# Weighted values of a windowed attention: FP32 products of PSUM weights, pair additions and gate products on GpSimd

## The chip, the cores and the metric

One core of one Trainium2 chip. The metric is the device time of the kernel in microseconds (us), median of several runs; the span in a profile, from the first to the last instruction, is about 2 us shorter. In the text PE is the matmul engine, DVE the vector engine, ACT the scalar engine and GpSimd (POOL in the profile) the fourth compute engine. PSUM (PS in the listings) is the memory in which PE's results land, used here in 8 banks; the other tiles named are in SBUF, the second memory of the core that the engines work on: VX holds values, ATX the softmax weights, PA to PC products of the two, SV added products, OT weighted values, HT hidden products, USX up projections, LOG and SM the softmax.

## The reference, cut to what matters

```python
# x: 2048 x 640, 32 heads of 20, window of 8 keys at distances 0, 2, ..., 14
xn = layernorm(x)
qkv = xn @ wqkv
attn = softmax(einsum("bhsd,bhswd->bhsw", q, kg) * scale)   # 8 weights a position
o = einsum("bhsw,bhswd->bhsd", attn, vg)                     # "weighted values"
# the second branch; its gate has no nonlinearity
h = (xn @ w_gate) * (xn @ w_up)                              # 2048 x 1536
return x + o @ wo + h @ w_down
```

## The kernel before: the parts that matter

The sequence is cut into 4 blocks of 512 positions. All instructions are put into one program order, and each engine works through its own part of it strictly in order (in after, a DVE product that could have run at 172.4 us stood until 177.05 behind a final addition that waited 4.23 us, see e13); semaphores are made from the buffers that operations share. The work of the second half is:

- 20 *units* of weighted values, 5 for each block of 512 positions. A unit multiplies 4 x 2 x 512 values by weights on DVE. The 128 partitions are 4 window groups x 32 heads, the factor 2 is the pair of *offset groups* (window positions 4 apart, called r), and PE sums the groups with a matrix of ones, 32 rows of output for each of 4 head dimensions.
- Gate and up projections: 24 groups of 5 matmuls a block on PE, evacuated by ACT, and 12 *gate products* a block (gate x up).
- The down projection of a block, 8 tiles of 17 matmuls. It needs the block's 12 gate products and its 5 units. I call the four dn0 to dn3.

```python
    def pv_mul(u):                                  # one DVE operation, bf16, both inputs in SBUF
        j = u // NCH
        v, p = VX[:, u % NVX], PB[u % NP]           # NP = 3 product buffers
        vw = bass.AP(v.tensor, v.offset, [v.ap[0], [VW, 4], [8, 2], [1, JB]])
        at = ATX[:, :, j * JB:(j + 1) * JB]
        a = at.unsqueeze(1).to_broadcast([128, 4, 2, JB])
        op("dve", lambda e: e.tensor_tensor(p[:], vw, a, ALU.mult), ...)

    def pv_sum(us):                                 # 16 matmuls for a pair of units
        for u in us:
            for r in range(2):
                for dq in range(4):                 # start at r == 0, stop at r == 1
                    op("pe", ... e.matmul(o, SEL[:], p[:, dq, r, :], ..., tile_position=(0, 32 * dq)))
        # ... ACT copies the sums into OT

    # what PE does, in this order; a small clock in the program decides
    # where the units and head sums are put between these entries
    add_gu(0); add_gu(1); add_dn(0); add_gu(2); add_dn(1); add_gu(3); add_dn(2); add_dn(3)
```

The hidden products live in two buffers (`HT[:, j % 2]`), so the gate groups of block 2 can't start before dn0 has read block 0. The up projections wait in 6 small buffers (`USX`) for their gate product.

Of the kernel before, what the change touches and what calls it, by code (L numbers as in the profile page):

```python
# [3 lines left out]
FP32 = mybir.dt.float32  # L4
BF16 = mybir.dt.bfloat16
ACT = mybir.ActivationFunctionType
ALU = mybir.AluOpType
# [3 lines left out]
NCH = 5  # L11
# [10 lines left out]
JB = 512  # L22
# [5 lines left out]
VW = JB + 8  # L28
# [9 lines left out]
class Sched:  # L38
# [47 lines left out]
    def op(self, eng, fn, r=(), w=(), dma=False, name=""):  # L86
        X = _Op()
        X.eng, X.fn, X.name, X.dma = eng, fn, name, dma
        X.needs_tick, X.event, X.pre_know, X.idx = False, None, None, len(self.ops)
        rk = [k for a in r for k in self.keys(a)]  # L90
        wk = [k for a in w for k in self.keys(a)]
        deps = {}
        inorder = eng in ("pe", "act", "dve")
        for k in rk:
            st = self.state.get(k)
            if st is not None and st[0] is not None:
                deps[st[0].idx] = st[0]
        for k in wk:
            st = self.state.get(k)
            if st is None:  # L100
                continue
            o, rds = st
            if o is not None and not (eng == "pe" and o.eng == "pe"):
                deps[o.idx] = o
            for q in rds:
                if inorder and q.eng == eng and not q.dma:
                    continue
                deps[q.idx] = q
        last = {}
        keep = []  # L110
        for d in deps.values():
            if d.dma or d.eng == "pool":
                keep.append(d)
            else:
                b = last.get(d.eng)
                if b is None or b.idx < d.idx:
                    last[d.eng] = d
        X.deps = keep + list(last.values())
        for d in X.deps:
            if not d.dma:  # L120
                d.needs_tick = True
        for k in rk:
            st = self.state.get(k)
            if st is None:
                self.state[k] = [None, [X]]
            elif inorder and st[1] and st[1][-1].eng == eng and not st[1][-1].dma:
                st[1][-1] = X
            else:
                st[1].append(X)
        for k in wk:  # L130
            self.state[k] = [X, []]
        if dma:
            X.event = (self.nc.alloc_semaphore(f"dma{self.n_dma}"), 16)
            self.n_dma += 1
        self.ops.append(X)
        return X
# [59 lines left out]
def build_kernel(nc, A_x, A_wqkv, A_wo, B_x, B_w_gate, B_w_up, B_w_down, out):  # L196
    K = Sched(nc)
    op = K.op
# [3 lines left out]
    def sb(name, shape, dtype=BF16, at=None):  # L202
        n = mybir.dt.size(dtype)
        for s in shape[1:]:
            n *= s
        n = (n + 63) // 64 * 64
        if at is None:
            at = place[0]
            place[0] += n
        assert at + n <= 229344, (name, at + n)  # L210
        return K.sbuf(name, shape, dtype, at)
# [9 lines left out]
    a_qk = place[0]  # L221
    place[0] += 2 * DH * VW * 2
    QT = sb("QT", [128, NCH, S], at=a_qk)
    KT = sb("KT", [128, NCH, VL], at=a_qk + NCH * S * 2)
    NVX = 8
    VX = sb("VX", [128, NVX, 4, VW], at=a_qk)
    a_ra = place[0]
    HT = sb("HT", [128, 2, NF, JB])
    WQKV = sb("WQKV", [128, 3, NCH, D], at=a_ra)
    a_pr = place[0]  # L230
    NPW = 6
    PRD = sb("PRD", [128, NPW, S])
    PB = [sb("PA", [128, 4, 2, JB], at=a_pr), sb("PB", [128, 4, 2, JB], at=a_pr + 8 * JB * 2),
          sb("PC", [128, 4, 2, JB], at=a_qk + NVX * 4 * VW * 2)]
    NP = len(PB)
    ATX = sb("ATX", [128, 2, S], at=a_pr + 2 * 8 * JB * 2)
    MX = sb("MX", [128, 4, JB], at=a_pr)
    MY = sb("MY", [128, 2, JB], at=a_pr + 4096)
# [20 lines left out]
    SEL = sb("SEL", [128, 32])  # L259
    G = sb("G", [128, NCH, H])  # L260
    PS = nc.alloc_psum_tensor("PS", [128, 8, 512], FP32)
# [6 lines left out]
    def dma(o, i, r=(), w=(), name="", eng="sp"):  # L268
        return op(eng, lambda e: e.dma_start(o, i), r=r, w=w, dma=True, name=name)  # L269
# [7 lines left out]
       r=[IDENT[:]], w=[IDENT[:]], name="ident")  # L277
# [3 lines left out]
       r=[G[:]], w=[G[:]], name="g1")  # L281
    op("pool", lambda e: e.affine_select(G[:], G[:], pattern=[[128, NCH], [-DH, H]], compare_op=ALU.is_ge,
                                         fill=0.0, base=0, channel_multiplier=1),
       r=[G[:]], w=[G[:]], name="g2")
# [89 lines left out]
    bank_ring = list(range(6))  # L374
# [116 lines left out]
    def attn_move(j):  # L491
        for wq in range(4):
            src = LOG[32 * j:32 * j + 32].rearrange("p (r q) s -> p r q s", r=2)[:, :, wq, :]
            dst = ATX[32 * wq:32 * wq + 32, :, j * JB:(j + 1) * JB]
            dma(dst, src, r=[src], w=[dst], name=f"atx{j}_{wq}")
# [5 lines left out]
        dma(dst, src, r=[("vscr", m, q) for m in range(NCH + 1) for q in range(4)], w=[dst], name=f"vx{u}")  # L501


    def pv_mul(u):
        j = u // NCH
        v, p = VX[:, u % NVX], PB[u % NP]
        vw = bass.AP(v.tensor, v.offset, [v.ap[0], [VW, 4], [8, 2], [1, JB]])
        at = ATX[:, :, j * JB:(j + 1) * JB]
        a = at.unsqueeze(1).to_broadcast([128, 4, 2, JB])
        op("dve", lambda e: e.tensor_tensor(p[:], vw, a, ALU.mult), r=[v, at], w=[p[:]], name=f"pv{u}")  # L510
        if u + NVX < NU:
            vx_load(u + NVX)

    def pv_sum(us):
        for u in us:
            b, p = 6 + u % 2, PB[u % NP]
            for r in range(2):
                for dq in range(4):
                    o = PS[32 * dq:32 * dq + 32, b, :]
                    op("pe", (lambda o, p, dq, r: lambda e: e.matmul(o, SEL[:], p[:, dq, r, :], start=(r == 0), stop=(r == 1),  # L520
                                                                  tile_position=(0, 32 * dq)))(o, p, dq, r),
                       r=[SEL[:], p[:, dq, r, :]], w=[o], name=f"I{u}_{dq}_{r}")
        for u in us:
            j, c = divmod(u, NCH)
            b = 6 + u % 2
            o = OT[:, c, j * JB:(j + 1) * JB]
            op("act", (lambda o, b: lambda e: e.activation(o, PS[:, b, :], ACT.Copy))(o, b), r=[PS[:, b, :]], w=[o],  # L527
               name=f"oev{u}")
# [2 lines left out]
    pair_ctr = [0]  # L531
    h_pending = []
    h_keep = [1]

    def flush_h(keep):
        n = 0
        while len(h_pending) > keep:
            h_pending.pop(0)()
            n += 1
        return n  # L540

    def glu(which, m, j):
        k = pair_ctr[0] % NUS
        T = (WG, WU)[which]
        h = HT[:, j % 2, m, :]
        o = (h, USX[:, k, :])[which]
        b = bank()
        for c in range(NCH):
            l, x = T[:, c, m * 128:(m + 1) * 128], XNT[:, c, j * JB:(j + 1) * JB]
            op("pe", (lambda l, x, c: lambda e: e.matmul(PS[:, b, :], l, x, start=(c == 0), stop=(c == NCH - 1)))(l, x, c),  # L550
               r=[l, x], w=[PS[:, b, :]], name=f"gu{which}_{m}_{j}_{c}")
        op("act", lambda e: e.activation(o, PS[:, b, :], ACT.Copy), r=[PS[:, b, :]], w=[o], name=f"guev{which}_{m}_{j}")  # L552
        if which == 1:
            pair_ctr[0] += 1
            h_pending.append(lambda: op("dve", lambda e: e.tensor_tensor(h, h, o, ALU.mult), r=[h, o], w=[h],  # L555
                                        name=f"h{m}_{j}"))
            return 0.43 * flush_h(h_keep[0])
        return 0.0

    def xr_load(t):  # L560
# [58 lines left out]
    for t0 in (0, 2):  # L619
        bm = bank()  # L620
        for which in (0, 1):
            for t in (t0, t0 + 1):
                b = bank()
# [8 lines left out]
    for t0 in (4, 6, 8, 10):  # L632
        bm = None
        for g in range(5):
            b = bank()
# [12 lines left out]
    NU = NJ * NCH  # L648
    t_pe, t_dve = [40.0], [41.0]
# [3 lines left out]
    for q in range(4):  # L653
        a, b = SEL[32 * q:32 * q + 32, :], IDENT[32 * q:32 * q + 32, 32 * q:32 * q + 32]
# [14 lines left out]
    units_done = [0]  # L669
# [17 lines left out]
    def run_fill(until):  # L687
        while t_pe[0] < until and pos[0] < len(fill):
            it = fill[pos[0]]
            if it[0] == "dn":  # L690
                if units_done[0] < NCH * (it[1] + 1):
                    return
                t_pe[0] += 2.31
                it[2]()
            else:
                t_pe[0] += it[0]
                d = it[1]()
                t_dve[0] += d if isinstance(d, float) else 0.0
            pos[0] += 1
# [4 lines left out]
    batch, ready = [], None  # L704
    for i, (w, c) in enumerate(order):
# [6 lines left out]
        if ready is not None and len(batch) == 2:  # L712
# [6 lines left out]
            ready = None  # L719
        if len(batch) == 4:  # L720
            ready = (batch, t_dve[0] + 0.2)
# [4 lines left out]
    t_dve[0] = max(t_dve[0], t_pe[0] + 2.5)  # L726
    for u in range(NVX):
        vx_load(u)
    bank_ring[:] = bank_ring + [4, 5]
    h_keep[0] = NUS - 1  # L730
    for cost, st in softmax_steps():
        st()
# [2 lines left out]
    h_keep[0] = 1  # L735
    for j in range(NJ):
        attn_move(j)
    t_dve[0] += 3.0
    for u in range(0, NU, 2):
        pv_mul(u)  # L740
        if u:
            run_fill(t_ready)
            pv_sum((u - 2, u - 1))
            t_pe[0] = max(t_pe[0], t_ready) + 1.13
            units_done[0] += 2
        pv_mul(u + 1)
        t_dve[0] += 4.57
        t_ready = t_dve[0] + 0.2
    run_fill(t_ready)
    pv_sum((NU - 2, NU - 1))  # L750
    units_done[0] += 2
    while pos[0] < len(fill):
        run_fill(1e9)
    K.emit(stores)
# [35 lines left out]
```

## Time and profile before

| | before |
|---|---|
| device time | 289.2 us |
| PE busy | 275.4 of 287.3 us |
| DVE busy, GpSimd busy | 171.4, 2.3 us |
| product of one unit (DVE) | 2.29 us |
| dn0 starts | 146.95 us |

The page's first parts, kernel before: busy time and share of the span for each engine, then the span in 40 slices of 7.2 us with the busy share in tenths, and the clock granted to PE.

```profile
PE 275.4 (96%) x1968; PEld 156.7 (55%) x1986; DVE 171.4 (60%) x260; ACT 116.1 (40%) x211; POOL 2.3 (1%) x17
...
PE   7899999999999999998997999999999999999996
...
DVE  5776792999999768859994999521222112222221
...
POOL 2000000000000000000000000000000000000000
PEclk9999999999999999999999799999999999999999
```

PE is the limit; counted from 0, DVE is full in slices 7 to 12, where it multiplies queries and keys, and again in most of 18 to 24 (about 129 to 180 us), where the units run; GpSimd does next to nothing.

Costliest groups, kernel before, by form: engine, operation, output<-inputs, partitions x elements, count, then busy us, mean ns, and idle time before them with its releaser.

```profile
L432 DVE TENSOR_TENSOR PRD<-QT,KT 128x2048 bf16<-128x2048 bf16 x40 | 45.8, 1220 | 5.0 <-ACT KT L390 4.2
...
L510 DVE TENSOR_TENSOR PA<-VX,ATX 128x4096 bf16<-128x4096 bf16 x7 | 16.0, 2285 | 4.0 <-DMA ATX<-LOG 4.0
...
L555 DVE TENSOR_TENSOR HT<-HT,USX 128x512 bf16<-128x512 bf16 x48 | 19.1, 420 | 39.5 <-ACT USX L552 39.5
```

Windows, kernel before, one for each stage of PE (end of softmax; rest of block 1; dn0; block 2; dn1).

```profile
105.00:125.00 20.00, 19.95 (x93) 9.10 (x93) 15.11 (x20) 14.04 (x21) 0.00 (x0) 1.00 0.27 85
125.00:147.00 22.00, 20.64 (x128) 8.56 (x129) 21.41 (x21) 11.67 (x22) 0.00 (x0) 1.00 0.66 195
147.00:175.00 28.00, 25.89 (x218) 15.30 (x218) 24.24 (x20) 5.73 (x11) 0.00 (x0) 0.94 0.54 158
175.00:203.00 28.00, 27.68 (x149) 11.97 (x150) 11.47 (x15) 16.35 (x28) 0.00 (x0) 1.00 0.04 12
203.00:222.00 19.00, 18.95 (x139) 13.60 (x139) 4.19 (x9) 0.60 (x1) 0.00 (x0) 1.00 0.16 53
```

The columns are the window, its length, then busy us (and instructions) of PE, PE's weight loads, DVE, ACT and GpSimd, the granted clock, the DMA share and GB/s. Up to dn0 (second line) PE and DVE are both almost full; afterwards DVE has more and more room, and PE loses only about 2 us in the dn0 stage.

Two moments of the timeline of before (start, duration, engine, operation): a softmax step, and dn0's first 12 matmuls.

```profile
115.07 1.22 DVE L455 TENSOR_TENSOR SM<-LOG 128x1024 f32<-128x1024 bf16 x1
...
146.95 1.79 PE L576 MATMUL PS<-WD,HT 128*128 128x320 bf16 x12
```

### The profile page before, as it was taken

The page shows a single profiled execution, that of the slowest core. Times are in us where ns is not written, and L with a number is a line of the kernel's source. Part 1 is how long each engine was busy: PE and PEld are TensorE (multiplying, and loading weights), DVE is VectorE, ACT ScalarE, POOL GpSimd, SP SyncE. Part 2 cuts the span into 40 slices and gives each one's busy share as a digit, 9 for nine tenths or more (in the row PEclk, how much of TensorE's full clock was granted, in tenths as well). Part 3 has the DMA queues.
Part 4 walks back from the last instruction along what each step waited for, and adds up shares of the span by engine and source line. Part 5 has one row for each costly group of instructions (what it writes and reads, how often), then busy time and mean ns, then how long its engine had stood idle before and what let it go on. Part 6 is the DMA issues. An engine that isn't in the chain of part 4 may idle for free.

```text
span 287.3 us, 4706 instructions
## 1 busy us (share of the span) xinstructions
PE 275.4 (96%) x1968; PEld 156.7 (55%) x1986; DVE 171.4 (60%) x260; ACT 116.1 (40%) x211; POOL 2.3 (1%) x17
## 2 busy tenths in 40 slices
PE   7899999999999999998997999999999999999996
PEld 3789887443434344443453564444676444677774
DVE  5776792999999768859994999521222112222221
ACT  2355556544644479525732034655200555300000
POOL 2000000000000000000000000000000000000000
PEclk9999999999999999999999799999999999999999
DMA  6824999007989692035976731000021100012211
GB/s 199 281 72 66 396 389 256 3 2 302 392 335 391 217 356 65 0 76 140 307 221 190 208 105 50 2 0 0 2 91 48 46 0 0 2 63 73 74 43 46
DMA packets 30468, 39.57 MB, mean 138 GB/s; under 512 B 4464, under 2 KB 26608, under 8 KB 30448
## 3 DMA queue, kind: packets, MB, share of 16 engines
q1 hardware_dynamic: 30448, 39.29, 41.5%
q8 instruction: 15, 0.25, 0.3%
q14 instruction: 5, 0.04, 0.0%
HBM read 25.07 MB, written 13.16 MB: 133 GB/s over the span
## 4 chain that ended last, share of the span: by engine, by line
PE 72%; DVE 15%; DMA 4%; issue 4%; ACT 2%; SPq 2%; DVEq 0%; ACTq 0%
PE PS L550 27%; PE PS L576 19%; PE PS L385 11%; PE PS L404 7%; PE PS L440 3%; DVE PC L510 3%; DVE PB L510 3%; DMA XST<-in_A_x_dram 2%; PE PS L397 2%; DVE PA L510 2%; SPq L269 2%; DVE SM L455 2%; DMA XR<-in_A_x_dram 1%; PE PS L360 1%; DVE RS L468 1%
## 5 line engine op out<-in xcount | busy, mean ns | idle before, releaser
L550 PE MATMUL PS<-XNT,WU 128*128 128x512 bf16 x238 | 59.4, 379 | 1.4 <-ACT USX L552 1.2
L576 PE MATMUL PS<-WD,HT 128*128 128x320 bf16 x384 | 59.0, 304 | 0.0
L550 PE MATMUL PS<-XNT,WG 128*128 128x512 bf16 x229 | 57.5, 379 | 0.7 <-issue 0.5
L432 DVE TENSOR_TENSOR PRD<-QT,KT 128x2048 bf16<-128x2048 bf16 x40 | 45.8, 1220 | 5.0 <-ACT KT L390 4.2
L576 PEld LDWEIGHTS PS<-WD,HT 128*128 128x128 bf16 x384 | 37.8, 99 | 17.2 <-issue 1.7
L552 ACT ACTIVATE HT<-PS 128x512 bf16<-128x512 f32 x48 | 29.1, 605 | 39.6 <-PE PS L550 39.6
L580 DVE TENSOR_TENSOR FOUT<-PS,XR 128x320 bf16<-128x320 f32 x32 | 15.4, 490 | 46.2 <-PE PS L576 42.5
L555 DVE TENSOR_TENSOR HT<-HT,USX 128x512 bf16<-128x512 bf16 x48 | 19.1, 420 | 39.5 <-ACT USX L552 39.5
L550 PEld LDWEIGHTS PS<-XNT,WU 128*128 128x128 bf16 x240 | 23.3, 98 | 30.1 <-ACT USX L552 1.7
L552 ACT ACTIVATE USX<-PS 128x512 bf16<-128x512 f32 x48 | 28.9, 603 | 26.3 <-PE PS L550 18.3
L550 PEld LDWEIGHTS PS<-XNT,WG 128*128 128x128 bf16 x240 | 22.9, 98 | 29.5 <-issue 1.7
L385 PE MATMUL PS<-XNT,WQKV 128*128 128x512 bf16 x145 | 32.8, 379 | 0.4 <-issue 0.3
L576 PE MATMUL PS<-WO,OT 128*128 128x320 bf16 x160 | 27.1, 300 | 0.0
L385 PEld LDWEIGHTS PS<-XNT,WQKV 128*128 128x128 bf16 x150 | 14.1, 98 | 18.8 <-ACT VST L390 2.1
L404 PE MATMUL PS<-XNT,WQKV 128*128 128x256 bf16 x200 | 23.6, 273 | 0.0
L404 PEld LDWEIGHTS PS<-XNT,WQKV 128*128 128x128 bf16 x200 | 19.1, 98 | 2.0
L527 ACT ACTIVATE OT<-PS 128x512 bf16<-128x512 f32 x20 | 11.1, 600 | 22.3 <-PE PS L520 22.1
L576 PEld LDWEIGHTS PS<-WO,OT 128*128 128x128 bf16 x160 | 15.8, 99 | 6.3
L510 DVE TENSOR_TENSOR PA<-VX,ATX 128x4096 bf16<-128x4096 bf16 x7 | 16.0, 2285 | 4.0 <-DMA ATX<-LOG 4.0
L390 ACT ACTIVATE VST<-PS 128x512 bf16<-128x512 f32 x20 | 12.0, 599 | 14.3 <-PE PS L385 14.3
L510 DVE TENSOR_TENSOR PB<-VX,ATX 128x4096 bf16<-128x4096 bf16 x7 | 16.0, 2285 | 0.2 <-PE PS L520 0.2
L510 DVE TENSOR_TENSOR PC<-VX,ATX 128x4096 bf16<-128x4096 bf16 x6 | 13.7, 2285 | 0.2 <-PE PS L520 0.2
(52 smaller groups left out, 166.5 us busy)
## 6 DMA issues: line engine op xcount, KB each, us to landing
VX<-v_scratch SPq DMA_DIRECT2D x20, 520.0 KB, 5.0
v_scratch<-VST SPq DMA_DIRECT2D x20, 512.0 KB, 4.5
XST<-in_A_x_dram SPq DMA_DIRECT2D x16, 160.0 KB, 4.6
XR<-in_A_x_dram SPq DMA_DIRECT2D x16, 160.0 KB, 2.4
out_dram<-FOUT SPq DMA_DIRECT2D x16, 160.0 KB, 1.8
WG<-in_B_w_gate_dram SPq DMA_DIRECT2D x1, 1920.0 KB, 12.0
WU<-in_B_w_up_dram SPq DMA_DIRECT2D x1, 1920.0 KB, 16.4
WD<-in_B_w_down_dram SPq DMA_DIRECT2D x1, 1920.0 KB, 22.6
```

What stands on the lines that cost most here:

```text
L385: op("pe", (lambda l, x, c: lambda e: e.matmul(PS[:, b, :], l, x, start=(c == 0), stop=(c == NCH - 1)))(l, x, c), r=[l, x], w=[PS[:, b, :] ...
L390: op("act", lambda e: e.activation(o, PS[:, b, :], ACT.Copy), r=[PS[:, b, :]], w=[o], name=f"pev{which}_{m}_{j}")
L404: op("pe", (lambda l, x, c: lambda e: e.matmul(o, l, x, start=(c == 0), stop=(c == NCH - 1)))(l, x, c), r=[l, x], w=[o], name=f"pw{which}_ ...
L432: op("dve", lambda e: e.tensor_tensor(PRD[:, s, :], QT[:, c, :], k, ALU.mult), r=[QT[:, c, :], k], w=[PRD[:, s, :]], name=f"prod{w}_{c}")
L440: op("pe", (lambda o, x, j, c: lambda e: e.matmul(o, G[:, c, :], x, start=(c == 0), stop=(c == NCH - 1), tile_position=(0, 32 * j)))(o, x, ...
L510: op("dve", lambda e: e.tensor_tensor(p[:], vw, a, ALU.mult), r=[v, at], w=[p[:]], name=f"pv{u}")
L527: op("act", (lambda o, b: lambda e: e.activation(o, PS[:, b, :], ACT.Copy))(o, b), r=[PS[:, b, :]], w=[o], name=f"oev{u}")
L550: op("pe", (lambda l, x, c: lambda e: e.matmul(PS[:, b, :], l, x, start=(c == 0), stop=(c == NCH - 1)))(l, x, c), r=[l, x], w=[PS[:, b, :] ...
L552: op("act", lambda e: e.activation(o, PS[:, b, :], ACT.Copy), r=[PS[:, b, :]], w=[o], name=f"guev{which}_{m}_{j}")
L555: h_pending.append(lambda: op("dve", lambda e: e.tensor_tensor(h, h, o, ALU.mult), r=[h, o], w=[h], name=f"h{m}_{j}"))
L576: op("pe", (lambda l, x, i: lambda e: e.matmul(PS[:, b, 0:DHALF], l, x, start=(i == 0), stop=(i == n - 1)))(l, x, i), r=[l, x], w=[PS[:, b ...
L580: op("dve", lambda e: e.tensor_tensor(o, PS[:, b, 0:DHALF], xr, ALU.add), r=[PS[:, b, :], xr], w=[o], name=f"fin{t}_{nb}")
```

## The change

The intent: PE is the limit, so halve its head sums. The products become FP32, GpSimd adds the two offset groups and rounds once to bf16, and PE sums 4 instead of 8 matmuls a unit. So that DVE's products and GpSimd's work don't exclude each other (in e1 three gate products on DVE took 4.49 us beside GpSimd's adds, 1.1 in before), the weights are copied to PSUM by ACT, and each product has only one SBUF input. The gate products "of the last two blocks" move to GpSimd too. The PSUM copies take two banks, and the FP32 buffers leave room for 5 instead of 8 value buffers. Core of the diff:

```diff
-    NVX = 8
+    NVX = 5
-    PB = [sb("PA", [128, 4, 2, JB], at=a_pr), ...]              # one unit each, bf16
+    PB = [sb("PA", [128, 2, 2, JB], FP32, at=a_pr), ...]        # half a unit each, FP32
+    def at_copy(j, r):                                          # ACT, SBUF -> PSUM banks 4 and 5
+        o, i = PS[:, 4 + r, :], ATX[:, r, j * JB:(j + 1) * JB]
     def pv_mul(u):
-        op("dve", lambda e: e.tensor_tensor(p[:], vw, a, ALU.mult), ...)
+        def mul(x, r0, nr): ... op("dve", ... e.tensor_tensor(p, vw, PSUM weights, ALU.mult))
+        def add(x): op("pool", ... e.tensor_tensor(o, p[:, :, 0, :], p[:, :, 1, :], ALU.add))
+        # two half units: mul, add, mul, add (first and last unit of a block in quarters)
     def pv_sum(us):
-            for r in range(2):
-                for dq in range(4): ... matmul of p[:, dq, r, :]
+            for dq in range(4): ... matmul of SV[:, dq, :]
-            h_pending.append(lambda: op("dve", ... e.tensor_tensor(h, h, o, ALU.mult)))
+            h_pending.append(lambda: op(h_eng[0], ... e.tensor_tensor(h, h, o, ALU.mult)))
-    bank_ring[:] = bank_ring + [4, 5]
+    h_eng[0] = "pool"                      # when the softmax has been issued
     # the plan: 4.66 us a unit on DVE, 4.7 on GpSimd, nothing there for gate products
```

More of the change, by code (lines that the diff above doesn't have):

```diff
@@ L232, in build_kernel @@
     PRD = sb("PRD", [128, NPW, S])
-    PB = [sb("PA", [128, 4, 2, JB], at=a_pr), sb("PB", [128, 4, 2, JB], at=a_pr + 8 * JB * 2),
-          sb("PC", [128, 4, 2, JB], at=a_qk + NVX * 4 * VW * 2)]
+    a_vx = a_qk + NVX * 4 * VW * 2
+    PB = [sb("PA", [128, 2, 2, JB], FP32, at=a_pr), sb("PB", [128, 2, 2, JB], FP32, at=a_pr + 8 * JB * 2),
+          sb("PC", [128, 2, 2, JB], FP32, at=a_vx)]
     NP = len(PB)
+    SV = [sb(f"SV{i}", [128, 4, JB], at=a_vx + 8 * JB * 2 + i * 4 * JB * 2) for i in range(3)]
+    NSV = len(SV)
     ATX = sb("ATX", [128, 2, S], at=a_pr + 2 * 8 * JB * 2)
@@ L501, in vx_load, with slot, mul, add @@
         dma(dst, src, r=[("vscr", m, q) for m in range(NCH + 1) for q in range(4)], w=[dst], name=f"vx{u}")
+    def at_copy(j, r):
+        o, i = PS[:, 4 + r, :], ATX[:, r, j * JB:(j + 1) * JB]
+        op("act", lambda e: e.activation(o, i, ACT.Copy), r=[i], w=[o], name=f"atp{j}_{r}")
     def pv_mul(u):
-        j = u // NCH
-        v, p = VX[:, u % NVX], PB[u % NP]
-        vw = bass.AP(v.tensor, v.offset, [v.ap[0], [VW, 4], [8, 2], [1, JB]])
-        at = ATX[:, :, j * JB:(j + 1) * JB]
-        a = at.unsqueeze(1).to_broadcast([128, 4, 2, JB])
-        op("dve", lambda e: e.tensor_tensor(p[:], vw, a, ALU.mult), r=[v, at], w=[p[:]], name=f"pv{u}")
+        j, c = divmod(u, NCH)
+        def slot(x):
+            return PB[(2 * u + x) % NP]
+        def mul(x, r0, nr):
+            v, p = VX[:, u % NVX, 2 * x:2 * x + 2, :], slot(x)[:, :, r0:r0 + nr, :]
+            vw = bass.AP(v.tensor, v.offset + 8 * r0, [v.ap[0], [VW, 2], [8, nr], [1, JB]])
+            at = PS[:, 4 + r0:4 + r0 + nr, :]
+            a = at.unsqueeze(1).to_broadcast([128, 2, nr, JB])
+            op("dve", lambda e: e.tensor_tensor(p, vw, a, ALU.mult), r=[v, at], w=[p], name=f"pv{u}_{x}_{r0}")
+        def add(x):
+            o, p = SV[u % NSV][:, 2 * x:2 * x + 2, :], slot(x)
+            op("pool", lambda e: e.tensor_tensor(o, p[:, :, 0, :], p[:, :, 1, :], ALU.add), r=[p[:]], w=[o],
+               name=f"pva{u}_{x}")
+        if c in (0, NCH - 1):
+            for r in range(2):
+                if c == 0:
+                    at_copy(j, r)
+                for x in range(2):
+                    mul(x, r, 1)
+            for x in range(2):
+                add(x)
+        else:
+            for x in range(2):
+                mul(x, 0, 2)
+                add(x)
         if u + NVX < NU:
@@ L515, in pv_sum @@
         for u in us:
-            b, p = 6 + u % 2, PB[u % NP]
-            for r in range(2):
-                for dq in range(4):
-                    o = PS[32 * dq:32 * dq + 32, b, :]
-                    op("pe", (lambda o, p, dq, r: lambda e: e.matmul(o, SEL[:], p[:, dq, r, :], start=(r == 0), stop=(r == 1),
-                                                                  tile_position=(0, 32 * dq)))(o, p, dq, r),
-                       r=[SEL[:], p[:, dq, r, :]], w=[o], name=f"I{u}_{dq}_{r}")
+            b, p = 6 + u % 2, SV[u % NSV]
+            for dq in range(4):
+                o = PS[32 * dq:32 * dq + 32, b, :]
+                op("pe", (lambda o, p, dq: lambda e: e.matmul(o, SEL[:], p[:, dq, :], start=True, stop=True,
+                                                           tile_position=(0, 32 * dq)))(o, p, dq),
+                   r=[SEL[:], p[:, dq, :]], w=[o], name=f"I{u}_{dq}")
         for u in us:
@@ L533, in build_kernel @@
     h_keep = [1]
+    h_eng = ["dve"]
     def flush_h(keep):
@@ L554, in glu @@
             pair_ctr[0] += 1
-            h_pending.append(lambda: op("dve", lambda e: e.tensor_tensor(h, h, o, ALU.mult), r=[h, o], w=[h],
+            h_pending.append(lambda: op(h_eng[0], lambda e: e.tensor_tensor(h, h, o, ALU.mult), r=[h, o], w=[h],
                                         name=f"h{m}_{j}"))
-            return 0.43 * flush_h(h_keep[0])
+            return 0.43 * flush_h(h_keep[0]) * (h_eng[0] == "dve")
         return 0.0
@@ L737, in build_kernel, with run_to @@
         attn_move(j)
+    h_eng[0] = "pool"
     t_dve[0] += 3.0
-    for u in range(0, NU, 2):
-        pv_mul(u)
-        if u:
-            run_fill(t_ready)
-            pv_sum((u - 2, u - 1))
-            t_pe[0] = max(t_pe[0], t_ready) + 1.13
-            units_done[0] += 2
-        pv_mul(u + 1)
-        t_dve[0] += 4.57
-        t_ready = t_dve[0] + 0.2
-    run_fill(t_ready)
-    pv_sum((NU - 2, NU - 1))
-    units_done[0] += 2
+    t_pool = t_dve[0]
+    sums = []
+    def run_to(t):
+        while sums and sums[0][0] <= t:
+            ready, us = sums.pop(0)
+            run_fill(ready)
+            pv_sum(us)
+            t_pe[0] = max(t_pe[0], ready) + 0.7
+            units_done[0] += len(us)
+        run_fill(t)
+    for u in range(NU):
+        run_to(t_dve[0])
+        pv_mul(u)
+        t_dve[0] += 4.66
+        t_pool = max(t_pool + 4.7, t_dve[0] + 2.4)
+        if u % 2 == 1:
+            sums.append((t_pool, (u - 1, u)))
+    run_to(1e9)
     while pos[0] < len(fill):
```

## The prediction

> **What bounds it now.** The matmul engine (PE): 275.4 of 287.3 us busy (page, part 1), 72% of the chain that ended last. Between 125 and 185 us (windows by stage), where the 20 units of weighted values run, PE is busy 56.3 of 60, DVE 53.7. A bf16 product of a unit takes 2.29 us on DVE, 2.20 from start to start; a pair's head sums take 0.98 us of PE plus gaps (timeline). PE reaches the first down projection (dn0) at 146.9. DVE paces little after that: one 1.95 us wait at 156, after which the granted clock is 0.83 (window 155 to 165).
>
> **What the change does.**
> - Head sums: 8 instead of 16 matmuls a pair, about 0.5 us each over 10 pairs: -5 us of PE. Gate products that queued behind DVE's first products (PE idle 1.6 around 132) leave DVE: -1.5 us.
> - DVE: 4,096 FP32 products a unit [...]. An FP32 result of 1,024 elements takes 1.22 us in this trace, 512 0.69: 2.2 us per half unit, 4.5 a unit instead of 2.2.
> - GpSimd: no such operation is in the trace. [...] The program plans 4.7 a unit, nothing for gate products.
> - The label says the last two blocks' products move. By the code all products pending when the first unit starts move: 3 of block 0, all of block 1, blocks 2 and 3: 39 of 48. GpSimd is in order, so block 1's lie between the adds.
>
> **On the critical path.** dn0 now cannot start before units 0-5 are added and summed, and nothing can fill PE: block 2 needs the hidden buffers that dn0 frees. First product about 126 (weights land at 125.1, one PSUM copy 0.6). PE finishes block 1 at about 144. GpSimd has 12 adds and 8 interleaved gate products from 129.5[...], so dn0 starts near 167 instead of 147. With gate products free it would still be about 156. Over block 2, [...] slack won during dn0 absorbs part, I expect 5-10 us more waiting at later head sums. [...]
> After dn0 starts: 32 down tiles x 2.31 = 73.9, 48 gate groups x 1.08 = 51.8, 7 sum pairs x 0.6 = 4, [...] waits 6: 139. 167 + 139 = 306 for PE's end; before, PE's end 284.5 went with 289.2. So about 311 us.
>
> **Range.** 298 to 323; faster by over 2%: 3%, within: 8%, slower: 89%.
>
> **What would show it.** [...] DVE products 2.2-2.3 us with waits on GpSimd. PE idle 15-25 us before dn0, released by GpSimd; granted clock below 0.9 just after. The chain of waits turns to GpSimd between 126 and 167.
>
> **What would make it wrong.** A faster GpSimd (adds of 1.5, products of 0.6 would leave DVE's 4.5 a unit as pace: about 293). Or contention: [...] gate products during the softmax could delay its end [...] (no trace here shows it).

(The sum came to 311 us: GpSimd's 12 adds and 8 gate products from 129.5 put dn0 at 167, then 139 to PE's end and 4.7 from there to the time. Of the 139, 73.9 + 51.8 + 4 + 6 is 135.7; the restart term and rounding are the rest.)

## The result, and the profile after

After: 324.68 us median (324.5 to 326.9, 4 runs); before in the same rounds: 289.22. The ratio is 1.1247, 95% interval 1.1213 to 1.1281. (Ratios and intervals here are from the fast runs of the same rounds, so not quite the ratio of the medians.) The direction and the main mechanism (dn0 waits for GpSimd's queue) were as predicted; the time lies 1.7 us above the stated range and 13.7 above the predicted 311.

The page's first parts, kernel after:

```profile
PE 282.7 (88%) x1889; PEld 158.1 (49%) x1906; DVE 205.8 (64%) x257; ACT 120.8 (37%) x219; POOL 141.3 (44%) x96
...
PE   7799999999999999748317998979597999999996
...
DVE  5667866999994895787574999957559500011211
...
POOL 2000000000000064299999779999999745510000
PEclk9999999999999999995855999999779999999999
```

GpSimd has become the engine with the nines just where PE has its holes, and PE's granted clock is lower in and after the first holes (0.76 from 131 to 172 us, 0.91 from 172 to 196, by the windows below).

The groups of after that answer to those shown of before (the full form of the products, the adds and the gate products):

```profile
L522 DVE TENSOR_TENSOR PA<-VX,PS 128x2048 f32<-128x2048 bf16 x8 | 18.3, 2283 | 1.5 <-POOL SV L526 1.5
...
L526 POOL TENSOR_TENSOR SV<-PA 128x1024 bf16<-128x1024 f32 x14 | 33.0, 2355 | 9.7 <-DVE PA L522 9.7
...
L585 POOL TENSOR_TENSOR HT<-HT,USX 128x512 bf16<-128x512 bf16 x39 | 46.8, 1212 | 28.9 <-ACT USX L582 28.8
```

A half unit on DVE took 2.28 us (2.2 predicted), an add 2.36, a gate product 1.21, and 39 gate products moved, not 24, as predicted. The longest wait of PE, from the list of waits of after:

```profile
PE PS L549 <- POOL SV L526: 29.0, 15, 4.0
```

PE waited 29.0 us in 15 waits for GpSimd's adds, at its head sums. Windows by PE's stages, kernel after (same columns; the stages now begin at 131, 172, 196, 232, 257):

```profile
131.00:172.00 41.00, 20.53 (x83) 7.40 (x84) 31.46 (x20) 13.52 (x25) 37.05 (x21) 0.76 0.38 107
172.00:196.00 24.00, 22.64 (x154) 14.33 (x152) 19.77 (x19) 3.59 (x6) 19.34 (x9) 0.91 0.45 125
196.00:232.00 36.00, 28.91 (x143) 12.30 (x144) 28.93 (x19) 18.51 (x32) 35.70 (x20) 0.98 0.30 87
232.00:257.00 25.00, 23.18 (x154) 14.67 (x156) 16.87 (x16) 1.96 (x4) 23.96 (x13) 0.89 0.13 41
```

In the first and third of these GpSimd is busy for 37.05 of 41 and 35.70 of 36 us. The starts of PE's stages, read from both timelines:

| | before | after | change of the stage's length |
|---|---|---|---|
| dn0 starts | 146.95 | 172.21 | +25.3 |
| block 2's gate groups start | 174.86 | 196.26 | -3.9 |
| dn1 starts | 203.00 | 232.46 | +8.1 |
| block 3's gate groups start | 221.69 | 257.16 | +6.0 |
| dn2 starts | 247.37 | 282.84 | 0.0 |
| end of the span | 287.3 | 322.7 | 0.0 |

(Each change is the difference of the two lengths of the stage that ends there, except in the first row, where it is everything up to dn0.) The 3.9 us that dn0's stage became shorter are mostly not the halving: only two pairs' head sums (16 matmuls, 2.0 us) fall into it, where before has five pairs (80 matmuls, 5.2 us) and a PE wait of 1.95 at 156; the other pairs moved to later stages. From dn0 on, all head sums, counted from start to start less the listed waits, take 6.9 us of PE in after and 7.5 in before: issued in pieces as the adds come, half the matmuls save 0.5 us. (In e12 below the same 56 matmuls, issued 8 at a time, take 4.0.) From block 3 on the two kernels are the same.

GpSimd's timeline of after, before dn0, shows the queue that paces it, and above it two operations from the end of the softmax:

```profile
116.65 2.17 DVE L458 TENSOR_TENSOR SM<-LOG 128x1024 f32<-128x1024 bf16 x1
...
117.91 1.92 POOL L585 TENSOR_TENSOR HT<-HT,USX 128x512 bf16<-128x512 bf16 x1 [0.17 <-ACT USX L582]
...
134.79 2.36 POOL L526 TENSOR_TENSOR SV<-PA 128x1024 bf16<-128x1024 f32 x1 [7.98 <-DVE PA L522]
137.11 2.36 POOL L526 TENSOR_TENSOR SV<-PB 128x1024 bf16<-128x1024 f32 x1
139.43 2.27 POOL L585 TENSOR_TENSOR HT<-HT,USX 128x512 bf16<-128x512 bf16 x2
...
169.26 2.35 POOL L526 TENSOR_TENSOR SV<-PC 128x1024 bf16<-128x1024 f32 x1
172.21 3.38 PE L606 MATMUL PS<-WD,HT 128*128 128x320 bf16 x12
```

From 134.8 on: two adds, two gate products, two adds, and so on with one gap of 0.16 us, until the twelfth add, at 169.26, completes unit 5, and after its head sum dn0 can start. The softmax step took 2.17 us where the same step of before took 1.22, with a gate product beside it that took 1.92 instead of about 1.15. That is the first thing that the predicted sum didn't hold: the first product of a unit starts at 131.23, predicted about 126.

### The profile page after: what moved, and what is told of

It is laid out like the page before. It is cut to its first block, busy times and chain, and to the rows that moved or that the text cites. A ratio compares the mean times of both kernels' runs of the same rounds, so it can differ in the third digit from the quotient of the medians.

```text
span 322.7 us, 4631 instructions
## 1 busy us (share of the span) xinstructions
PE 282.7 (88%) x1889; PEld 158.1 (49%) x1906; DVE 205.8 (64%) x257; ACT 120.8 (37%) x219; POOL 141.3 (44%) x96
## 4 chain that ended last, share of the span: by engine, by line
PE 51%; POOL 25%; DVE 11%; DMA 6%; issue 4%; ACT 2%; SPq 1%; DVEq 0%
POOL SV L526 18%; PE PS L606 16%; PE PS L580 13%; PE PS L388 10%; POOL HT L585 7%; PE PS L407 6%; PE PS L443 3%; DMA out_dram<-FOUT 2%; DMA XST<-in_A_x_dram 2%; PE PS L400 2%; DVE SM L458 2%; DVE PC L522 1%; SPq L272 1%; DVE PA L522 1%; PE PS L363 1%
## 5 line engine op out<-in xcount | busy, mean ns | idle before, releaser
L580 PE MATMUL PS<-XNT,WU 128*128 128x512 bf16 x239 | 61.0, 387 | 0.2
L606 PE MATMUL PS<-WD,HT 128*128 128x320 bf16 x384 | 60.9, 311 | 0.0
L585 POOL TENSOR_TENSOR HT<-HT,USX 128x512 bf16<-128x512 bf16 x39 | 46.8, 1212 | 28.9 <-ACT USX L582 28.8
L522 DVE TENSOR_TENSOR PA<-VX,PS 128x1024 f32<-128x1024 bf16 (+1 forms) x20 | 32.9, 1643 | 12.0 <-ACT PS L509 7.0
L549 PE MATMUL PS<-SV,SEL 128*32 128x512 bf16 x80 | 12.5, 426 | 29.2 <-POOL SV L526 29.0
L526 POOL TENSOR_TENSOR SV<-PA 128x1024 bf16<-128x1024 f32 x14 | 33.0, 2355 | 9.7 <-DVE PA L522 9.7
L522 DVE TENSOR_TENSOR PC<-VX,PS 128x1024 f32<-128x1024 bf16 (+1 forms) x18 | 30.4, 1689 | 6.4 <-POOL SV L526 6.4
L522 DVE TENSOR_TENSOR PB<-VX,PS 128x1024 f32<-128x1024 bf16 (+1 forms) x18 | 30.4, 1689 | 3.4 <-POOL SV L526 2.8
L526 POOL TENSOR_TENSOR SV<-PC 128x1024 bf16<-128x1024 f32 x13 | 30.6, 2356 | 2.9 <-DVE PC L522 2.7
L526 POOL TENSOR_TENSOR SV<-PB 128x1024 bf16<-128x1024 f32 x13 | 30.6, 2356 | 0.7 <-DVE PB L522 0.7
```

The costliest lines, as they stand in the source:

```text
L522: op("dve", lambda e: e.tensor_tensor(p, vw, a, ALU.mult), r=[v, at], w=[p], name=f"pv{u}_{x}_{r0}")
L526: op("pool", lambda e: e.tensor_tensor(o, p[:, :, 0, :], p[:, :, 1, :], ALU.add), r=[p[:]], w=[o], name=f"pva{u}_{x}")
L549: op("pe", (lambda o, p, dq: lambda e: e.matmul(o, SEL[:], p[:, dq, :], start=True, stop=True, tile_position=(0, 32 * dq)))(o, p, dq), r=[ ...
L580: op("pe", (lambda l, x, c: lambda e: e.matmul(PS[:, b, :], l, x, start=(c == 0), stop=(c == NCH - 1)))(l, x, c), r=[l, x], w=[PS[:, b, :] ...
L585: h_pending.append(lambda: op(h_eng[0], lambda e: e.tensor_tensor(h, h, o, ALU.mult), r=[h, o], w=[h], name=f"h{m}_{j}"))
L606: op("pe", (lambda l, x, i: lambda e: e.matmul(PS[:, b, 0:DHALF], l, x, start=(i == 0), stop=(i == n - 1)))(l, x, i), r=[l, x], w=[PS[:, b ...
```

## The experiments

14 kernels ran, in the order below; each was timed in 3 rounds beside before.

| run | what it is | us | dn0 starts | from dn0 to the end of the span |
|---|---|---|---|---|
| before | | 289.2 | 146.95 | 140.3 |
| after | | 324.68 | 172.21 | 150.5 |
| e1_gates_dve | all gate products back on DVE | 323.21 | 168.47 | 152.1 |
| e2_gates_label | only blocks 2 and 3 on GpSimd | 322.07 | 168.36 | 151.4 |
| e3_softmax_free | the six beside the softmax back on DVE | 320.11 | 167.35 | 152.1 |
| e4_dve_pace | no GpSimd at all, bf16 products of PSUM weights | 299.46 | 156.53 | 141.1 |
| e5_gates_psum | gate products on DVE from PSUM | 320.19 | 166.46 | 152.7 |
| e6_before_gates_pool | before, gate products on GpSimd | 301.90 | 154.51 | 145.5 |
| e7_half_from6 | before, half sums by DVE adds from unit 6 | 285.95 | 146.81 | 137.3 |
| e8_half_all | the same for all units | 294.12 | 155.83 | 136.1 |
| e9_no_gates | after without the 39 gate products | 302.20 | 159.16 | 141.0 |
| e10_gates_no_adds | e4, gate products on GpSimd | 296.92 | 153.83 | 140.9 |
| e11_warm | after with dummy matmuls in the waits | 325.62 | 171.04 | 152.8 |
| e12_half_paced | e7 with another order | 284.99 | 145.58 | 137.7 |
| e13_fin_later | after, final additions later on DVE | 321.77 | 171.21 | 148.2 |
| e14_half_paced2 | e12 with yet another order | 286.92 | 145.52 | 139.0 |

The last two columns are of the one profiled run of each kernel, the time is the median of four. (For e5 it is the median of three: its run of 324.47 us is over 1.5% above its fastest and counts as slow.)

### e1: gate products back on DVE

```diff
-    h_eng[0] = "pool"
```

> After, with all gate products left on DVE; the adds stay on GpSimd. Theory (GpSimd's in-order queue of adds plus gate products sets the start of the first down projection and the waits in block 2; softmax products delay the first unit): first product back at about 126.4 us instead of 131.2, first down projection at about 161 instead of 172.2 (now paced by DVE), no waits of 10 us at the head sums of block 2: about 301 us. Rival 1 (the FP32 products on DVE [...] are the main cost, the gate products hardly matter): 315 or more. Rival 2 (most of the loss is a granted clock that stays low): first down projection near 161 but still over 310 us.

Measured 323.21 us, dn0 at 168.47. My theory (301 us) as written fell: GpSimd had no gate products any more and the time hardly moved. The time alone fits both rivals (315 or more; over 310), but rival 2 wanted dn0 near 161, and rival 1's reason, that DVE's products are the main cost and the gate products hardly matter, falls with e4 (299.46 us) and e9 (302.20 us without the gate products) below. The timelines of DVE and GpSimd show why the time hardly moved:

```profile
130.91 4.49 DVE L585 TENSOR_TENSOR HT<-HT,USX 128x512 bf16<-128x512 bf16 x3
...
132.25 2.53 POOL L526 TENSOR_TENSOR SV<-PB 128x1024 bf16<-128x1024 f32 x1
137.68 2.36 POOL L526 TENSOR_TENSOR SV<-PC 128x1024 bf16<-128x1024 f32 x1 [2.90 <-DVE PC L522]
```

Three gate products that take 1.1 us of DVE in before took 4.49 here: they stood until the two adds on GpSimd, from 129.94 to 134.78, were over. The product behind them came late, and then GpSimd was idle for 2.90 us waiting for it. The mean gate product on DVE rose from 0.42 to 0.89 us. A gate product has two SBUF inputs. In these runs such an operation on DVE and a GpSimd operation excluded each other: the gate products here beside the adds, the softmax step of after beside a gate product on GpSimd (2.17 us, 1.22 in before), and the unit products of e6 beside gate products on GpSimd (3.24, 2.28 alone). The two kinds of work were serial here whichever of the two engines ran the gate products. The author's care, weights in PSUM, kept the products of values clear of it (2.28 us with GpSimd's adds here, 2.28 without in e4), but not the gate products.

### e2: what the label says

```diff
-op(h_eng[0], lambda e: e.tensor_tensor(h, h, o, ALU.mult) ...
+op("pool" if j >= 2 else "dve", lambda e: e.tensor_tensor(h, h, o, ALU.mult) ...
```

> After, with only the products of blocks 2 and 3 on GpSimd, as the label of the change says; those of blocks 0 and 1 on DVE. Theory: first down projection at about 161 us as in e1, but the waits of block 2 (about 10 us and a slower restart of 2 to 3) remain: about 313 us. If the waits after the first down projection came from something else than the gate products, e2 equals e1.

Measured 322.07 us against the 313 expected, dn0 at 168.36 instead of 161: the mean of the 24 gate products on DVE was 0.81 us. So before dn0 e2 is what e1 is; from dn0 to the end e2, e1 and after (151.4, 152.1, 150.5) are too close to tell apart. The alternative, "e2 equals e1", came true by its words, but it too rested on gate products that are free on DVE, which e1 refuted; so e2 says nothing about what the waits after dn0 come from.

### e3: the softmax undisturbed

```diff
         run_to(t_dve[0])
+        h_eng[0] = "pool"        # was set before the loop
         pv_mul(u)
```

> After, with only the first six moved gate products (those that GpSimd ran beside the softmax) back on DVE. Theory (two-input DVE work and GpSimd work block each other): softmax steps back at 1.21 us, end of softmax at 121 instead of 125.8, first product near 126.4, all later work 4.7 earlier: about 320 us. If there is no such blocking: 324.7.

Measured 320.11 us, as the theory said. The softmax step is back at 1.22 us (at 115.06), the first product at 126.37 instead of 131.23, dn0 at 167.35. The six gate products beside the softmax cost 4.6 us of the total (324.68 - 320.11).

### e4: DVE's slower product alone

```diff
-    PB = [sb("PA", [128, 2, 2, JB], FP32, ...), ...]       # three FP32 half units
+    PB = [sb(f"P{i}_{k}", [128, 2, 2, JB], ...) ...]        # six bf16 half units
-                add(x)                                     # no additions
-    h_eng[0] = "pool"
 # pv_sum: the loop over r again, 16 matmuls a pair
```

> After without GpSimd: bf16 products of SBUF values and PSUM weights, 16 head-sum matmuls a pair as before, gate products on DVE. It leaves the slower DVE product alone. Theory: products still about 2.2 us for 2048 elements (4.5 a unit) though the output is bf16, first down projection at about 158.5 us, total about 299.5. If the FP32 output was what made them slow, products fall to about 1.1 us and the total to about 290.

Measured 299.46 us, dn0 at 156.53. The group of the products in their full form:

```profile
L522 DVE TENSOR_TENSOR P<-VX,PS 128x2048 bf16<-128x2048 bf16 x24 | 53.7, 2279 | 0.0
```

The products took 2.28 us for 2,048 elements, though their output is bf16; with both inputs in SBUF, 2,048 bf16 elements take 1.22 us (L432 of before). So the weights in PSUM (FP32 there) were enough here to halve DVE's rate. It doesn't follow that the FP32 output is harmless: the softmax step shown above, with bf16 inputs in SBUF and FP32 output, takes 1.22 us for 1,024 elements, where the softmax's maximum of the same two inputs, with bf16 output, takes 0.69 (L455 of before), so about half the rate too. By these figures either part of the change alone would make the products slow; for the FP32 output this is an estimate from the softmax steps, no run has it without PSUM. In this form, before any GpSimd work, the change was bound to lose 10 us: the six units ahead of dn0 take twice as long on DVE. (e4 also keeps the PSUM copies, the 5 value buffers and the two lost banks; no run separates these, but neither DVE nor PE waits for value buffers or banks in its list of waits.)

### e5: gate products without a second SBUF input

```diff
-        op("act", ... copy of the up projection to USX)
+        if which == 1 and h_eng[0] == "pool": o = PS[:, b, :]   # no copy, DVE reads PSUM
```

> After, but from the first unit on the gate products run on DVE and read the up projection straight from PSUM (one SBUF input each, no ScalarE copy). e1 showed gate products on DVE stretched from 0.42 to 0.89 us in the mean beside GpSimd adds. Theory now (an operation with two SBUF inputs on DVE and a GpSimd operation exclude each other, so moving the products from one of these engines to the other gains nothing): products 0.69 us each with no stretching, adds back to back with the DVE products, first down projection at about 161.5 us, total about 308. If e1 was slow for another reason (DVE's plain load): first down projection at 168 or later, total 319 or more.

Measured 320.19 us. The exclusion was gone (gate products 0.684 us in the mean, none stretched; adds 2.35), but dn0 came at 166.46, not 161.5, so the time is a miss; by its total alone the rival (319 or more) fits. Now the two queues held each other up: in the list of waits DVE waited 26.2 us for up projections on PE, with products of units behind those gate products in its queue, and PE waited 11.3 us for banks that DVE had not read. It separates nothing about the total; it only confirms the exclusion by its absence. Against the rival, DVE's plain load, speaks e4: there DVE does the same products and all gate products, without adds beside them, and dn0 comes at 156.53.

### e6: the second clause of the change alone

```diff
 # before.py
-op("dve", lambda e: e.tensor_tensor(h, h, o, ALU.mult) ...
+op(h_eng[0], lambda e: e.tensor_tensor(h, h, o, ALU.mult) ...   # "pool" after the softmax
```

> Before, with the second clause of the change alone: gate products on GpSimd from the end of the softmax on. Theory of mutual exclusion: softmax ends about 4.7 us later as in after, bf16 products of two SBUF inputs stretched beyond 2.29 us by about 1.1 for each gate product, first down projection at about 155 instead of 147, total about 296. Without exclusion: products stay at 2.29, total 287 to 290.

Measured 301.90 us, dn0 at 154.51 (155 expected), total 6 us above the 296 expected, since the stretched products went on after dn0. Two lines of its timeline, DVE's product of a unit and GpSimd's gate products:

```profile
145.33 3.24 DVE L510 TENSOR_TENSOR PA<-VX,ATX 128x4096 bf16<-128x4096 bf16 x1
...
143.24 15.83 POOL L556 TENSOR_TENSOR HT<-HT,USX 128x512 bf16<-128x512 bf16 x5 [0.23 <-ACT USX L553]
```

A product went from 2.28 to 3.24 us and a gate product on GpSimd from 1.15 to about 3.2 (15.83 for 5): they take turns, one of each in 3.2 us (3.16 from start to start on DVE). Both lose.

### e7 and e8: half head sums where DVE has room, and everywhere

```diff
 # before.py, pv_mul; NHALF = 6 in e7, 0 in e8
+        if u >= NHALF:
+            op("dve", lambda e: e.tensor_tensor(p[:, :, 0, :], p[:, :, 0, :], p[:, :, 1, :], ALU.add), ...)
 # pv_sum: r only 0 for these units, start and stop set
```

> Before, with half the head sums only for units 6 to 19: DVE adds the two offset groups in bf16 in place after its bf16 product. Units 0 to 5, on which the first down projection waits, stay as before. Theory (units are late before the first down projection only; after it there is slack, so DVE work there is free and the saved matmuls count): add 1.22 us, 7 pairs x 0.45 us saved, first down projection still at 147, total about 285.5. Rival (DVE is so full in this stage that any longer unit delays PE): 290 or more.

> Before, with half the head sums for all 20 units by DVE adds in bf16. Theory: units 0 to 5 take 3.4 us each instead of 2.2, first down projection about 5 us later (152), then the same 3 us saved: about 291 us. If the first six units do not decide it, e8 equals e7 or is faster.

e7: 285.95 us, ratio to before 0.9892 (interval 0.9868 to 0.9915): a real gain of about 3.3 us, as expected, by a plain bf16 add of 1.23 us on DVE. e8: 294.12 us, 3 us above its forecast. From dn0 to the end e8 is even 1 us shorter than e7, and all that it loses, it loses before dn0 (155.83 against 146.81). DVE's waits for PE to free a product buffer before dn0 (2.17 us at 141, 1.45 at 152) are about as long as e8's miss; that they are its cause is not tested. (e7, e8, e12 and e14: their intervals exclude 1.) So the intent of the change was sound and worth 3 us; what counts is that units 0 to 5 are not made longer.

### e9 and e10: the gate products left out; the adds left out

```diff
 # e9: the change without the 39 products (wrong on purpose)
-op(h_eng[0], lambda e: e.tensor_tensor(h, h, o, ALU.mult) ...
+None if h_eng[0] == "pool" else op("dve", lambda e: e.tensor_tensor(h, h, o, ALU.mult) ...
 # e10: e4, with h_eng[0] = "pool" set at the first unit
```

> After with the 39 moved gate products left out altogether (a wrong result on purpose). e1 and e5 put them elsewhere and each brought a new cost, so their own share is still unmeasured. Theory (the adds alone fit into DVE's pace; the gate products on top are most of the loss): first product at 126.4 us, first down projection at about 156.5, no waits of 10 us in block 2, total about 295. Rival (the adds alone, with the order of PE's head sums, do it): 310 or more.

> e4 (products of PSUM weights on DVE, no adds on GpSimd, 16 head-sum matmuls) with the gate products on GpSimd from the first unit on. DVE's products have one SBUF input, so they should not exclude them. Theory: products stay 2.2 us, gate products 1.15, first down projection at about 154 (e4: 156.5, less the gate products that DVE no longer does), total about 296. If gate products on GpSimd are harmful by themselves: 305 or more.

e9: 302.20 us. Without the 39 gate products, and so without the exclusion in the softmax, 22.5 of the 35.5 us are gone (324.68 - 302.20 of 324.68 - 289.22); the FP32 products and adds are the other 13. It is 7 us above the forecast for two reasons: dn0 came at 159.16, because the adds alone, back to back at 2.31 us, are a little slower than DVE and end later; and from dn0 to the end it took as long as e4 with twice the head-sum matmuls, 141.0 us: the head sums take 6.4 us of PE there against 8.2 in e4, but PE's waits, 3.8 us for adds against 2.5 for products, ate most of that. One caution: e9 *passed* the comparison with the reference. The second branch is so small in these inputs that the comparison does not see 39 missing products. Its passing therefore says nothing of the moved products in the other kernels either; that they are right rests on their unchanged expression and their dependencies.

GpSimd's gate products in e10:

```profile
L583 POOL TENSOR_TENSOR HT<-HT,USX 128x512 bf16<-128x512 bf16 x33 | 38.0, 1153 | 115.6 <-ACT USX L580 115.6
```

e10: 296.92 us, as expected (296). With one-SBUF-input products and no adds, the 33 gate products on GpSimd took 1.153 us and did no harm; it is even faster than e4. So neither GpSimd nor the gate products there are bad in themselves. On GpSimd the adds and the gate products share one queue, on DVE the gate products and the adds exclude each other (e1), and their sum is too much.

### e11: PE's clock kept up

```diff
 # pv_sum of the change: matmuls on zeros before pieces of the head sums that PE waits for
+                for _ in range(nw): ... e.matmul(PS[:, bank_ring[0], :], ZERO[:, 0:128], ZERO[:]) ...
```

> After with dummy matmuls on zeros in PE's waits before the head sums, so that its clock is not lowered. Theory (the waits cost their own length, and the lowered clock after them only 4 to 5 us: first tiles of the first and second down projection take 3.4 and 1.2 to 1.5 us instead of 1.8 and 0.8): granted clock above 0.98, total about 320.3. If the lowered clock were most of the loss: below 310.

Measured 325.62 us at a clock of 1.000 (after: 0.952). dn0's first 12 matmuls were back at 1.80 us (after: 3.38), its stage 1.9 us shorter than in after, yet dn1 started at 232.67 against 232.46. A miss: the lowered clock shows no cost here, where GpSimd decides when the next head sums can run. My prediction had it as a term of the sum. (The dummies may overshoot a wait, by at most 1.7 us each time, so this is not exact.)

### e12 and e14: can the better kernel be ordered better?

```diff
 # e12, from e7
-        t_dve[0] += 4.57 + (2.4 if u >= NHALF else 0.0)
+        t_dve[0] += 4.57 + (3.5 if u >= NHALF else 0.0)
     t_dve[0] += 3.0
+    run_fill(t_dve[0])
 # e14, from e12: 2.9 instead of 3.5, and t_dve[0] += 0.45 for each tile of a down projection
```

> e7 with the gate products that are pending flushed before the first unit (PE waited 1.2 us for them at 132) and the head sums of units 6 to 19 planned 1.1 us a pair later (PE waited 2.6 us for a DVE add at 167). Theory: both waits go, total about 283 us. If those waits only move: 286.

> e12 with DVE's final additions counted in the plan (0.45 us a tile), so that the head sums of units 8 to 11 stand later in PE's queue; e12 still waited 3.0 us for a DVE add at 169 and 1.2 behind it. Theory: these go, total about 281.5 us. If the waits only move: 285.

e12: 284.99 us, ratio to before 0.9845 (0.9826 to 0.9863), the best, by 4.3 us; but 2 us short of its forecast. The first wait went, the second stayed: PE waited 3.0 us at 169 for a DVE add. e14: 286.92 us; that wait fell to 0.4 but a wait of 3.5 us for a bank behind a final addition came. So those waits move with the order, as the rival said.

### e13: what GpSimd lost during dn0

```diff
 # tail() of the change: the final addition (dn result + x on DVE) of dn0 and dn1 is issued two tiles later
-        op("dve", ... e.tensor_tensor(o, PS[:, b, 0:DHALF], xr, ALU.add) ...)
+        fin_pending.append(fin); flush_fin(2 if t < 8 else 0)
```

> After, with each final addition of the first two down projections issued on DVE two tiles later. In after, GpSimd idled 5.0 us during the first down projection because DVE's next product stood in its queue behind a final addition that waited 4.2 us for PE's first tile, and GpSimd was then the limit until the head sum at 231.9 us. Theory: most of these 5 us of GpSimd come back, and with GpSimd the limit of block 2 PE reaches the second down projection 3 to 5 us earlier (228 to 229.5 instead of 232.5), total 320 to 321.5. If the waits in block 2 are not GpSimd's lost time: 324.7.

In after, DVE's and GpSimd's timelines at the start of dn0 read:

```profile
176.64 0.49 DVE L610 TENSOR_TENSOR FOUT<-PS,XR 128x320 bf16<-128x320 f32 x1 [4.23 <-PE PS L606]
177.05 2.28 DVE L522 TENSOR_TENSOR PC<-VX,PS 128x2048 f32<-128x2048 bf16 x1
...
179.41 2.36 POOL L526 TENSOR_TENSOR SV<-PC 128x1024 bf16<-128x1024 f32 x1 [2.08 <-DVE PC L522]
```

The product at 177.05 could have run at 172.4; it stood behind a final addition that waited for PE's first tile, and GpSimd ran dry. In the whole stage GpSimd idled 5.0 us, time that it could not make up in block 2. In e13 the idle time fell to 1.0 us and dn1 started at 227.38, 5.1 us earlier than in after (expected 228 to 229.5); 1.0 of the 5.1 was there at dn0 already (171.21). The total, 321.77, 2.9 less than after's, is 0.3 above the expected range, as dn1's stage took 26.4 us instead of 24.7.

## Why the prediction was wrong, point by point

The predicted sum was 167 (start of dn0) + 139 (from there to PE's end) + 4.7 (as before from PE's end to the time) = 311. Measured: 172.2 + 147.7 + 4.8 = 324.7.

- **GpSimd's durations: no trace of before shows such an operation.** Measured: an add of 1,024 elements 2.36 us in after, one every 2.31 in e9; gate products 1.15 each when undisturbed (e10).
- **39, not 24 gate products move: right,** from reading when the operation is issued, not when it is made.
- **"GpSimd has 12 adds and 8 interleaved gate products from 129.5", dn0 "near 167": right in what it counts and in its length, 37.5 us.** From the first add at 134.79 to the end of the twelfth at 171.61 are 36.8 us; dn0 follows at 172.21. The chain of waits of after goes through GpSimd there.
- **"First product about 126": the step that failed first, by 5.2 us.** It came at 131.23. The prediction named the cause among its risks ("gate products during the softmax could delay its end"), and left it out of the sum, though the six gate products in question were counted a few lines above. e3 measured it: 4.6 us of the time, with the first product back at 126.37. A risk that the program makes certain belongs in the sum.
- **"After dn0 starts: ... waits 6: 139": the second step that failed, by 8.7 us.** Matmuls of tiles and gate groups are the predicted 125.7. From dn0 on PE waits 10.0 us for adds, in 7 waits (29.0 in all, less 19.0 in 8 waits before dn0), not 6; the prediction's own text had "5-10 us more waiting", and its sum took 6. "Slack won during dn0 absorbs part" was wrong: GpSimd idled 5.0 us in that stage behind DVE's queue (in e13 dn1 came 5.1 us earlier, 4.1 of them after dn0). The restarts at dn0 and dn1 show 1.9 and 2.5 us of longer matmuls, 4.4 in all, more than the term; but by e11 taking them away shortens nothing (dn1 at 232.67 against 232.46), so this term doesn't belong in a sum in which another engine decides. What then remains of 147.7, 7.6 us, is mostly the head sums: 6.9 in pieces, against 4.
- **"With gate products free it would still be about 156": near.** 159.16 in e9.
- **"Gate products ... leave DVE: -1.5 us": not seen.** PE waited 2.1 us at 130 instead of 1.2 at 132 (by the list of waits; the prediction read 1.6), for ACT: the new PSUM copy stood in ACT's queue waiting 4.1 us for the weights, with an evacuation behind it.
- **What I had not thought of at all** is what e1 and e2 showed: that leaving the gate products on DVE would not have helped. As a forecast of after it did no harm, as an explanation it did: on my first theory e1 should have taken 301 us and took 323.

In short: of the 35.5 us lost, 22.5 go when the gate products are left out (e9), of which 4.6 are their exclusion of the softmax (e3). Most of these 22.5 belong to gate products and adds together, not to the gate products alone: without adds, gate products on GpSimd cost nothing (e10, 296.92, against e4, 299.46). The other 13 are 12.2 of later dn0, most of it DVE's halved rate (e4: 9.6), and no gain afterwards, because the halved sums come in pieces and wait for adds. Open is how the 10.0 us of waits of dn0, block 2 and dn1 divide between the adds' rate and the order of PE's queue; no run separates them.

## What to carry to other kernels

Before moving work to another engine, ask which stage decides and who has room *there*: the same halved head sums cost about 5 us when the first six units carry them too (e8) and gain 3 to 4 when they start after (e7, e12). Vector work with two SBUF inputs and GpSimd work were serial here (three gate products 4.49 us instead of 1.1 in e1, a unit product 3.24 instead of 2.28 in e6); moving the gate products from one to the other changed little as long as the adds stayed (e1, 323.21; e2, 322.07; after, 324.68), and a PSUM operand bought freedom at half the rate (2.28 us, not 1.22, for 2,048 bf16 elements). When an engine in strict order becomes the limit, count everything in its queue, and what sits ahead of its suppliers in theirs (e13).

## What the traces show of the engines

- GpSimd: an add from FP32 to bf16, 1,024 elements, 2.31 us from start to start (e9); a bf16 product of 512 elements, 1.15 us (e10).
- The exclusion looks like this in a profile: the blocked instruction is shown as busy and longer (DVE 1.22 to 2.17 us in after, 2.28 to 3.24 in e6; GpSimd 1.15 to about 3.2 in e6), not as idle. A RECIPROCAL on DVE, with one input, was not stretched by a gate product beside it (1.74 us at 122.39 in after, with the gate product at 123.24; 1.75 at 117.94 in before without one).
- PE's clock: in before, the window 155 to 165, with a wait of 1.95 us between sparse head sums, has a granted clock of 0.83, while e12, with one wait of 3.0 us, kept 1.000. No run here shows what decides.
